# A GELU feed-forward block on one core: the first chunk of x loaded in four quarters over two queues, b1 moved to GpSimd, and every turn of x put ahead of the first pass

## The chip, the cores and the metric

The kernel runs on one core of a Trainium2 chip. The metric is device time in microseconds (us) of one execution; a kernel's time is the median of its runs. The profile is that of one execution.

## What is computed

```python
B, S, D, F = 1, 2048, 448, 1792            # all bfloat16
def reference(x, w1, b1, w2, b2):
    h = jnp.einsum("bsd,df->bsf", x, w1) + b1
    h = gelu(h, approximate=True)
    return jnp.einsum("bsf,fd->bsd", h, w2) + b2
```

2048 tokens, each a row of 448 numbers, go through two matrix products with a GELU between them.

## The kernel before

**Two passes.** The 2048 tokens are cut into 4 chunks of 512, the 1792 hidden units into 14 tiles of 128. The first pass makes, for each of the 56 pairs of chunk and tile, a block of 128 hidden units by 512 tokens in one bank of PSUM, and ScalarE's Gelu (L366) adds b1 and writes it to `g_sb`. The second pass makes 16 output tiles of 128 tokens; VectorE adds b2 (L389), and SyncE stores them (the last part ScalarE). TensorE runs the whole first pass ahead of the second; the order is written out by hand and the five engines run their own lists, tied by semaphores.

**The first pass.** It needs x with its 448 features on the partitions. 448 is three and a half times 128, so x and w1 lie in four row blocks ("slots"), starting at rows 0, 128, 256 and 320. A step is two matmuls (L265) that serve two hidden tiles; in steps of full blocks (128 rows) both use the whole array, in the others each uses a half of it (64 rows). The first 8 hidden tiles have an order of their own, `OPEN`: steps 0 to 3 are slot 0 of tiles 0 to 3, each with one half of the chunk's tokens (256 columns): step 0 tiles 0 and 1, first half; step 1 tiles 2 and 3, first half; steps 2 and 3 the same with the second half. Step 4 is slot 0 of tiles 4 and 5 with all 512 columns, step 5 slot 1 of tiles 0 and 1, step 6 slot 1 of tiles 2 and 3, step 7 slot 0 of tiles 6 and 7. After that come the steps of half the array. What each step waits for is worked out in `opening_waits`: the piece of w1, the parts of x, and the banks of PSUM that parts of x still lie in.

**Turning x.** Chunks 1 to 3 of x are turned by DMA (`load_xT`). Chunk 0 is loaded as it lies, 128 partitions with four tokens each (`xn_sb`, index t = 0 to 3), and TensorE turns it: 16 matmuls of 128x128 against an identity matrix (L248), four for each t, one for each slot. The results lie in PSUM as six parts (`XPARTS`), each with a bank; VectorE or ScalarE casts a part to `xT_sb` once its last turn is done:

- part 0: first half of the tokens (t = 0, 1), slot 0, by VectorE
- part 1: first half, slot 1, by ScalarE
- part 2: first half, slots 2 and 3, by ScalarE
- part 3: second half (t = 2, 3), slot 0, by VectorE
- part 4: second half, slot 1, by VectorE
- part 5: second half, slots 2 and 3, by ScalarE

Turns run part by part: parts 0 to 4 (12 turns) ahead of the pass, part 5 (4 turns) ahead of step 2 (`XLATE`, `EARLY`). Ahead of them stand 12 warm-up matmuls on constants (L238).

**Loads, in the order of their issue on each queue.** SyncE (SP): the two halves of chunk 0 of x (L207, L208); slot 0 of w1 for tiles 4 to 7 (`load_w10(sp, 1)`); slots 1, 2, 3 of w1 for tiles 0 to 7 (L185); slots 0 to 2 (L186) and slot 3 (L189) of the rest of w1; chunks 1 to 3 of x, turned, four transfers each; w2 in two pieces; b2; then the stores. ScalarE: b1, as 14 rows of 128 (L355), then slot 0 of w1 for tiles 0 to 3 (`load_w10(act, 0)`), and behind them its table load (L358). GpSimd: the identity matrix (L224, L226), then 18 rows that fill up b1's block of 32 rows (L231). VectorE turns b1 (four 32x32 transposes, L383, and a cast, L385), behind its three casts of x and ahead of the b2 additions.

Of the kernel before, what the change touches and what calls it, by code (L numbers as in the profile page):

```python
# [11 lines left out]
def bass_standalone__dense_activation_gelu__prompt_kernel(  # L12
# [10 lines left out]
    P = 128  # L23
# [7 lines left out]
    STC = SC // P  # L31
    NFT = F // P

    KROW = [0, 128, 256, 320]
# [24 lines left out]
    W2_PIECES = [(0, 7), (7, 14)]  # L59


    XPARTS = [
        ("d", [(0, 0)]), ("a", [(0, 1)]), ("a", [(0, 2), (0, 3)]),
        ("d", [(1, 0)]), ("d", [(1, 1)]), ("a", [(1, 2), (1, 3)]),
    ]
    XBANK = [0, 2, 4, 5, 6, 7]

    XLATE = 5
    EARLY = 2

    SQ = 32
    NB = 8
# [48 lines left out]
    with ExitStack() as es:  # L121
# [4 lines left out]
        xn_sb = sb("xn_sb", [P, STC, D], BF16)  # L126
        ident = sb("ident", [P, P], BF16)
        act_junk = sb("act_junk", [P, 8], BF16)
        b1n_sb = sb("bin_sb", [SQ, P], BF16)
# [10 lines left out]
        sem_w1r = S_("sem_w1r")  # L140
        sem_w2 = [S_(f"sem_w2_{i}") for i in range(len(W2_PIECES))]
        sem_b2 = S_("sem_b2")
        sem_xn = [S_(f"sem_xn{i}") for i in range(2)]
        sem_b1n = S_("sem_b1n")
        sem_b1x = S_("sem_b1x")
        sem_x = [None] + [S_(f"sem_x{i}") for i in range(1, NSC)]
# [1 line left out]
        sem_xtp = S_("sem_xtp")  # L148
# [22 lines left out]
        def x_part(n, parts):  # L171
# [2 lines left out]
            src = ps[XBANK[n]][:, 0:2 * P * len(parts)]  # L174
            return to, src.rearrange("p (k t) -> p k t", k=len(parts))

        def load_w10(eng, i):
            a, b = W0_PIECES[i]
            with nc.allow_non_contiguous_dma(reason="w1 column pieces"):
                eng.dma_start(w1_sb[:, 0, a * P:b * P], w1[0:P, a * P:b * P]).then_inc(sem_w10[i], 16)  # L180
# [23 lines left out]

        @block.sync
        def _(sp):
            sp.dma_start(xn_sb[:, 0:2, :], x0_view[:, 0:2, :]).then_inc(sem_xn[0], 16)  # L207
            sp.dma_start(xn_sb[:, 2:4, :], x0_view[:, 2:4, :]).then_inc(sem_xn[1], 16)  # L208
            load_w10(sp, 1)
            load_w1(sp)  # L210
            load_xT(sp, 1)
            for c in range(2, NSC):
                load_xT(sp, c)
            for i in range(len(W2_PIECES)):
                load_w2(sp, i)
            sp.dma_start(b2_bc[:, :], b2.partition_broadcast(P)).then_inc(sem_b2, 16)
            for n in range(len(outs) - 1):
                sp.wait_ge(sem_osb, n + 1)
                store(sp, n)
            sp.wait_ge(sem_od, 16 * len(outs))  # L220

        @block.gpsimd
        def _(pool):
            pool.memset(ident[:, :], 0.0).then_inc(sem_id, 1)  # L224
            pool.wait_ge(sem_id, 1)
            pool.affine_select(  # L226
                out=ident[:, :], in_=ident[:, :], compare_op=ALU.not_equal, fill=1.0,
                base=0, pattern=[[-1, P]], channel_multiplier=1,
            ).then_inc(sem_id, 1)

            pool.dma_start(b1n_sb[NFT:SQ, :], w1[0:SQ - NFT, 0:P]).then_inc(sem_b1x, 16)  # L231

        @block.tensor
        def _(pe):
            ones_w = nc.const_aps.tensor(1.0, [P, P], BF16)
            ones_x = nc.const_aps.tensor(1.0, [P, WN], BF16)
            for _i in range(NWARM):
                pe.matmul(ps[0][:, 0:WN], lhsT=ones_w, rhs=ones_x, start=True, stop=True)  # L238
            pe.wait_ge(sem_id, 2)

            def turn_x(n):
                parts = XPARTS[n][1]
                for h, k in parts:
                    if (h, k) in ((0, 0), (1, 0)):
                        pe.wait_ge(sem_xn[h], 16)
                    for t in range(2):
                        col = parts.index((h, k)) * 2 * P + t * P
                        mm = pe.matmul(  # L248
                            ps[XBANK[n]][:, col:col + P],
                            lhsT=xn_sb[:, 2 * h + t, KROW[k]:KROW[k] + P],  # L250
                            rhs=ident[:, :],
                            start=True, stop=True,
                        )
                mm.then_inc(sem_xtp, 1)

            def free(kind, i):
                n = number[kind, i] - NB
                if n >= 0:
                    kind, i = jobs[n]
                    pe.wait_ge(sem_g if kind == "g" else sem_osb, i + 1)  # L260

            def rows(i, k, lo, hi, tokens, start, stop):
                c, ft = order[i]
                t0, t1 = tokens
                return pe.matmul(  # L265
                    bank("g", i)[:, t0:t1],
                    lhsT=w1_sb[lo:hi, k, ft * P:(ft + 1) * P],
                    rhs=xT_sb[lo:hi, k, c * SC + t0:c * SC + t1],
                    start=start, stop=stop,
                )  # L270

            met = set()

            def need(sem, value):
                if (sem.name, value) not in met:
                    pe.wait_ge(sem, value)
                    met.add((sem.name, value))

            def opening_waits(n):

                i, h, m, (t0, t1) = steps[n]
                slots = set(PHASES[h][m])
                for k in sorted(slots):
                    if k > 0:
                        need(sem_w1[k], 16)
                    else:
                        for p, (a, b) in enumerate(W0_PIECES):
                            if a <= i < b:
                                need(sem_w10[p], 16)
                for x, (e, parts) in enumerate(XPARTS):  # L290
                    if XBANK[x] in (i, i + 1) or any(
                        k in slots and t0 <= HALVES[half][0] < t1 for half, k in parts
                    ):
                        need(
                            sem_xTd if e == "d" else sem_xTa, sum(f == e for f, _ in XPARTS[:x + 1])
                        )

            def l1():
                for n, (i, h, m, tokens) in enumerate(steps):
                    if n == EARLY:  # L300
                        for x in range(XLATE, len(XPARTS)):
                            turn_x(x)
                    if n < N_OPEN:
                        opening_waits(n)
                    elif starts[n]:
                        if n == N_OPEN:
                            pe.wait_ge(sem_w1r, 32)
                        for t in (i, i + 1):
                            c, ft = order[t]
                            if c > 0 and ft == 0:  # L310
                                pe.wait_ge(sem_x[c], 16 * NKT)
                            free("g", t)
                    if turn[n] is not None:
                        pe.wait_ge(sem_turn, turned.index(turn[n]) + 1)
                    lower, upper = PHASES[h][m]
                    last = n in ends
                    if h == 2:
                        two = ((0, P, i, lower), (0, P, i + 1, upper))
                    else:
                        two = ((0, HALF, i + 1 - h, lower), (HALF, P, i + h, upper))  # L320
                    for lo, hi, tile, k in sorted(two, key=lambda one: one[2]):
                        mm = rows(tile, k, lo, hi, tokens, starts[n], last)
                        if last:
                            mm.then_inc(sem_l1, 1)
                    if n in turned:
                        mm.then_inc(sem_turn, 1)

            def l2(c):
                pe.wait_ge(sem_g, NFT * (c + 1))
                for n, (j, c0, c1) in enumerate(outs):  # L330
                    if j // STC != c:
                        continue
                    free("o", n)
                    for ft in range(NFT):
                        if j == 0:
                            for i, (a, _) in enumerate(W2_PIECES):
                                if ft == a:
                                    pe.wait_ge(sem_w2[i], 16)
                        mm = pe.matmul(  # L339
                            bank("o", n)[:, 0:c1 - c0],  # L340
                            lhsT=g_sb[:, ft, j * P:(j + 1) * P],
                            rhs=w2_sb[:, ft, c0:c1],
                            start=(ft == 0), stop=(ft == NFT - 1),
                        )
                    mm.then_inc(sem_l2, 1)

            for x in range(XLATE):
                turn_x(x)
            l1()
            for c in range(NSC):  # L350
                l2(c)

        @block.scalar
        def _(act):
            act.dma_start(b1n_sb[0:NFT, :], b1.rearrange("(c p) -> c p", p=P)).then_inc(sem_b1n, 16)  # L355
            load_w10(act, 0)
            zero = nc.const_aps.tensor(0.0, [P, 8], FP32)
            act.activation(act_junk[:, :], zero, ACT.Gelu_apprx_tanh)  # L358
# [62 lines left out]
```

## Time and profile before

| | us |
|---|---|
| runs | 94.48, 94.94, 95.01 (median 94.94) |
| the profiled execution | 93.88 |
| its span, first to last instruction | 92.1 |
| TensorE busy in the span | 89.1 |
| first warm-up starts | 0.79 |
| first turn of x starts | 3.53 |
| step 0 starts | 4.51 |
| last piece of the second pass ends in the chain | 89.88 |

The last four rows are points on the span's own clock, as are all times given as a point below. A matmul's row in the trace starts when the array takes it and ends when its last column has left, so that rows of successive matmuls overlap; the distance from start to start is the pace. A DMA has a row for its issue on the engine that issues it; when its data has landed is told by its semaphore.

Issue and landing of the loads in the opening:

| load | issued by | issue at | landed at |
|---|---|---|---|
| x, t = 0, 1 | SP | 0.75 | 3.39 |
| x, t = 2, 3 | SP | 1.20 | 4.01 |
| b1 | ScalarE | 0.76 | no landing recorded |
| b1's filling rows | GpSimd | 1.67 | 4.93 |
| w1 slot 0, tiles 0 to 3 | ScalarE | 1.43 | 4.36 |
| w1 slot 0, tiles 4 to 7 | SP | 1.66 | 5.19 |
| w1 slot 1, tiles 0 to 7 | SP | 2.13 | 5.96 |
| w1 slot 2, tiles 0 to 7 | SP | 2.60 | 6.60 |
| w1 slot 3, tiles 0 to 7 | SP | 3.08 | 7.63 |
| w1 rest, slots 0 to 2 | SP | 3.55 | 9.96 |
| w1 rest, slot 3 | SP | 4.03 | 10.60 |

### The profile page before, as it was taken

How to read it: one execution, taken by the hardware profiler on the slowest of the kernel's cores; microseconds unless marked ns; L12 is line 12 of the kernel's file. 1: busy time of each engine (PE TensorE's matmuls, PEld its weight loads, DVE VectorE, ACT ScalarE, POOL GpSimd, SP SyncE). 2: the span in 40 equal slices, each digit the busy share in tenths (PEclk: the TensorE clock that was granted, in tenths of full speed). 3: DMA queues.
4: the chain of work that ended last, by engine and by line, in shares of the span. 5: the costliest groups of instructions: out<-in, count | busy, mean ns of one | idle time of the engine just before them, and what ended most of it. 6: DMA issues, size and time to landing. Idle time of an engine off the chain costs nothing.

```text
span 92.1 us, 1498 instructions
## 1 busy us (share of the span) xinstructions
PE 89.1 (97%) x650; PEld 47.2 (51%) x650; DVE 12.2 (13%) x25; ACT 36.6 (40%) x61; POOL 1.4 (1%) x7
## 2 busy tenths in 40 slices
PE   6999999999999999999999999999999999999990
PEld 4664445555555555555545555555555555555570
DVE  0260000000000000000001112222211222222131
ACT  2640999877887779777973000000000000000000
POOL 5000000000000000000000000000000000000000
PEclk9999999999999999999999999999999999999999
DMA  1999988554893000000000111101111110011111
GB/s 24 343 332 333 154 148 73 114 108 74 271 368 104 0 0 4 7 0 0 0 0 0 50 57 50 42 7 50 50 50 50 50 50 29 28 50 50 50 50 50
DMA packets 12562, 7.52 MB, mean 82 GB/s; under 512 B 7171, under 2 KB 12172, under 8 KB 12556
## 3 DMA queue, kind: packets, MB, share of 16 engines
q1 hardware_dynamic: 12208, 7.26, 31.1%
q10 hardware_dynamic: 316, 0.17, 0.6%
q8 instruction: 5, 0.08, 0.3%
q0 software_dynamic: 32, 0.00, 0.1%
q14 instruction: 1, 0.01, 0.0%
HBM read 4.02 MB, written 1.84 MB: 64 GB/s over the span
## 4 chain that ended last, share of the span: by engine, by line
PE 97%; DVE 0%; issue 0%
PE ps L265 46%; PE ps L339 46%; PE ps L238 3%; PE ps L248 1%; DVE out_sb L389 0%
## 5 line engine op out<-in xcount | busy, mean ns | idle before, releaser
L265 PE MATMUL ps<-xT_sb,wi_sb 64*128 64x512 bf16 (+2 forms) x384 | 42.8, 374 | 0.0
L339 PE MATMUL ps<-wo_sb,g_sb 128*128 128x448 bf16 (+2 forms) x238 | 42.6, 341 | 0.0
L366 ACT ACTIVATE g_sb<-ps,bi_f 128x512 bf16<-128x512 f32 x56 | 33.7, 694 | 9.5 <-PE ps L265 9.5
L339 PEld LDWEIGHTS ps<-wo_sb,g_sb 128*128 128x128 bf16 x238 | 22.7, 98 | 20.1 <-issue 0.4
L265 PEld LDWEIGHTS ps<-xT_sb,wi_sb 64*128 64x128 bf16 (+1 forms) x384 | 21.7, 94 | 20.5 <-issue 0.6
L389 DVE TENSOR_TENSOR out_sb<-ps,bo_bc 128x448 bf16<-128x448 f32 (+2 forms) x17 | 10.1, 597 | 73.8 <-PE ps L339 73.8
L238 PE MATMUL ps<-const-bfloat16-1.0 128*128 128x256 bf16 x12 | 2.7, 413 | 0.8 <-PEq L406 0.8
L238 PEld LDWEIGHTS ps<-const-bfloat16-1.0 128*128 128x128 bf16 x12 | 1.6, 140 | 1.4 <-issue 0.8
L358 ACT ACT_TABLE_LOAD x1 | 1.3, 1283 | 1.8 <-issue 1.8
L362 ACT CAST xT_sb<-ps 128x512 bf16<-128x512 f32 (+1 forms) x3 | 1.4, 516 | 1.2 <-PE ps L248 1.2
L378 DVE CAST xT_sb<-ps 128x256 bf16<-128x256 f32 x3 | 1.2, 421 | 4.1 <-PE ps L248 3.9
L248 PEld LDWEIGHTS ps<-ident,xn_sb 128*128 128x128 bf16 x16 | 1.2, 112 | 0.5 <-issue 0.5
L248 PE MATMUL ps<-ident,xn_sb 128*128 128x128 bf16 x16 | 1.4, 244 | 0.0
L383 DVE STREAM_TRANSPOSE bit_sb<-bin_sb 32x32 bf16<-32x32 bf16 x4 | 0.8, 200 | 0.1
L231 POOL DMA_DIRECT2D bin_sb<-in_w_dram x1 | 0.7, 657 | 0.2 <-issue 0.2
L226 POOL TENSOR_SCALAR_AFFINE_SELECT ident<-ident 128x128 bf16<-128x128 bf16 x1 | 0.3, 287 | 0.2 <-POOL ident L224 0.2
L358 ACT ACTIVATE act_junk<-const-float32-0.0 128x8 bf16<-128x8 f32 x1 | 0.2, 209 | 0.0
L224 POOL MEMSET ident<- 128x128 bf16 x1 | 0.2, 204 | 0.3 <-POOLq L406 0.3
L385 DVE CAST bi_f<-bit_sb 128x14 f32<-128x14 bf16 x1 | 0.2, 176 | 0.0
L406 POOL MEMSET const-float32-0.0<- 128x1 f32 x1 | 0.1, 99 | 0.2 <-issue 0.2
L406 POOL MEMSET const-bfloat16-1.0<- 128x1 bf16 x1 | 0.1, 102 | 0.0
L406 POOL MEMSET const-uint8-127<- 128x1 uint8 x1 | 0.1, 102 | 0.0
(1 smaller groups left out, 0.1 us busy)
## 6 DMA issues: line engine op xcount, KB each, us to landing
out_dram<-out_sb SPq DMA_DIRECT2D x15, 112.0 KB, 1.7
wo_sb<-in_w_dram SPq DMA_DIRECT2D x2, 784.0 KB, 6.0
wi_sb<-in_w_dram SPq DMA_DIRECT2D x3, 256.0 KB, 4.0
wi_sb<-in_w_dram SPq DMA_DIRECT2D x1, 576.0 KB, 6.4
xn_sb<-in_x_dram SPq DMA_DIRECT2D x2, 224.0 KB, 2.7
wi_sb<-in_w_dram SPq DMA_DIRECT2D x1, 192.0 KB, 6.6
xT_sb<-in_x_dram SPq DMA_TRANSPOSE x12, 3.6
wi_sb<-in_w_dram ACTq DMA_DIRECT2D x1, 128.0 KB, 2.9
```

What stands on the lines that cost most here:

```text
L231: pool.dma_start(b1n_sb[NFT:SQ, :], w1[0:SQ - NFT, 0:P]).then_inc(sem_b1x, 16)
L238: pe.matmul(ps[0][:, 0:WN], lhsT=ones_w, rhs=ones_x, start=True, stop=True)
L248: mm = pe.matmul(ps[XBANK[n]][:, col:col + P], lhsT=xn_sb[:, 2 * h + t, KROW[k]:KROW[k] + P], rhs=ident[:, :], start=True, stop=True,)
L265: return pe.matmul(bank("g", i)[:, t0:t1], lhsT=w1_sb[lo:hi, k, ft * P:(ft + 1) * P], rhs=xT_sb[lo:hi, k, c * SC + t0:c * SC + t1], start= ...
L339: mm = pe.matmul(bank("o", n)[:, 0:c1 - c0], lhsT=g_sb[:, ft, j * P:(j + 1) * P], rhs=w2_sb[:, ft, c0:c1], start=(ft == 0), stop=(ft == NF ...
L358: act.activation(act_junk[:, :], zero, ACT.Gelu_apprx_tanh)
L362: act.copy(*x_part(n, parts)).then_inc(sem_xTa, 1)
L366: act.activation(g_sb[:, ft, c * SC:(c + 1) * SC], bank("g", i)[:, :], ACT.Gelu_apprx_tanh, bias=b1_f[:, ft:ft + 1], scale=1.0,).then_inc( ...
L378: dve.tensor_copy(*x_part(n, parts)).then_inc(sem_xTd, 1)
L383: dve.transpose(b1t_sb[to, :], b1n_sb[:, to]).then_inc(sem_b1T, 1)
L389: dve.tensor_tensor(out=out_sb[:, j, c0:c1], in0=bank("o", n)[:, 0:c1 - c0], in1=b2_bc[:, c0:c1], op=ALU.add,).then_inc(sem_osb, 1)
L406: nc = _bacc.Bacc("TRN2", target_bir_lowering=False, num_devices=1)
```

## The change

Chunk 0 of x comes as four transfers, one for each t, each with a semaphore: t = 0, 2 and 3 by SP, t = 1 by ScalarE. b1's 14 rows go from ScalarE's queue to GpSimd's, ahead of the filling rows. The turns run tile by tile, the four slots of t = 0, then those of t = 1, 2 and 3, all ahead of the first pass; each t waits for its own quarter. The parts, their banks, their casts and the order of the steps stay. A part is complete with its turn of t = 1 or t = 3.

```diff
-    XLATE = 5
-    EARLY = 2
...
-        sem_xn = [S_(f"sem_xn{i}") for i in range(2)]
+        sem_xn = [S_(f"sem_xn{i}") for i in range(STC)]
...
+        def load_x0(eng, t):
+            eng.dma_start(xn_sb[:, t, :], x0_view[:, t, :]).then_inc(sem_xn[t], 16)
...
         @block.sync
         def _(sp):
-            sp.dma_start(xn_sb[:, 0:2, :], x0_view[:, 0:2, :]).then_inc(sem_xn[0], 16)
-            sp.dma_start(xn_sb[:, 2:4, :], x0_view[:, 2:4, :]).then_inc(sem_xn[1], 16)
+            for t in (0, 2, 3):
+                load_x0(sp, t)
             load_w10(sp, 1)
             load_w1(sp)
...
+            pool.dma_start(b1n_sb[0:NFT, :], b1.rearrange("(c p) -> c p", p=P)).then_inc(sem_b1n, 16)
             pool.dma_start(b1n_sb[NFT:SQ, :], w1[0:SQ - NFT, 0:P]).then_inc(sem_b1x, 16)
...
             pe.wait_ge(sem_id, 2)
-            def turn_x(n):
-                parts = XPARTS[n][1]
-                for h, k in parts:
-                    if (h, k) in ((0, 0), (1, 0)):
-                        pe.wait_ge(sem_xn[h], 16)
-                    for t in range(2):
-                        col = parts.index((h, k)) * 2 * P + t * P
+            for t in range(STC):
+                pe.wait_ge(sem_xn[t], 16)
+                h = t // 2
+                for n, (_, parts) in enumerate(XPARTS):
+                    for b, (_, k) in enumerate(parts):
+                        if parts[b][0] != h:
+                            continue
+                        col = (2 * b + t % 2) * P
                         mm = pe.matmul(
                             ps[XBANK[n]][:, col:col + P],
-                            lhsT=xn_sb[:, 2 * h + t, KROW[k]:KROW[k] + P],
+                            lhsT=xn_sb[:, t, KROW[k]:KROW[k] + P],
                             rhs=ident[:, :],
                             start=True, stop=True,
                         )
-                mm.then_inc(sem_xtp, 1)
+                        if t % 2 == 1 and b == len(parts) - 1:
+                            mm.then_inc(sem_xtp, 1)
...
                 for n, (i, h, m, tokens) in enumerate(steps):
-                    if n == EARLY:
-                        for x in range(XLATE, len(XPARTS)):
-                            turn_x(x)
                     if n < N_OPEN:
...
-            for x in range(XLATE):
-                turn_x(x)
             l1()
...
         @block.scalar
         def _(act):
-            act.dma_start(b1n_sb[0:NFT, :], b1.rearrange("(c p) -> c p", p=P)).then_inc(sem_b1n, 16)
+            load_x0(act, 1)
             load_w10(act, 0)
```

## The prediction

> **What bounds the kernel now.** I read the page's busy shares first, then the chain that ended last in order of time, then the waits of the opening.
>
> ```profile
> span 92.1 us, 1498 instructions
> ...
> PE 89.1 (97%) x650; PEld 47.2 (51%) x650; DVE 12.2 (13%) x25; ACT 36.6 (40%) x61; POOL 1.4 (1%) x7
> ```
>
> TensorE is busy for 97% of the span, so only what moves its first or last work, or opens a hole in it, can move the end.
>
> ```profile
> 0.79 2.72 PE ps L238 x12
> ...
> 3.53 1.05 PE ps L248 x12
> 4.58 0.53 PE ps L265 x4
> 5.11 0.22 PE ps L248 x4
> 5.33 42.02 PE ps L265 x380
> 47.35 42.53 PE ps L339 x238
> ```
>
> Every piece is TensorE's (start, length, line): warm-ups (L238), 12 turns of x (L248), the first four matmuls of the first pass (L265), the last 4 turns, the rest of the first pass, the second pass (L339). From 5.33 to 89.88 there is nothing to win that this change touches. The opening is what it rearranges.
>
> ```profile
> PEld ps L265 <- DMA wi_sb<-in_w_dram: 0.6, 2, 0.3
> PEld ps L248 <- issue: 0.5, 1, 0.5
> ```
>
> These are waits of the weight loads, which run ahead of the matmuls; only part of them is TensorE's loss. I worked that out from matmul starts in the opening's timeline. The warm-ups start 0.213 us apart, the last at 3.09, so its slot ends at 3.30; the first turn starts at 3.53 (the first half of x landed at 3.39): 0.23 lost. The turns start 0.107 apart until 4.01, then 0.056: the array doubles its pace there, while the granted clock reads 1.00 throughout. The twelfth turn's slot ends at 4.42, the first L265 starts at 4.51: 0.09 lost to VectorE's cast. Then starts are on pace, except 0.10 at 7.12, where the matmul shape changes. So 0.23 + 0.09 = **0.32 us** is all that the profiled opening holds for this change, 0.34% of the time.
>
> ```profile
> 6.00 0.13 PEld L265 LDWEIGHTS ps<-xT_sb,wi_sb 128*128 128x128 bf16 x2 [0.30 <-DMA wi_sb<-in_w_dram]
> ...
> 10.64 0.13 PEld L265 LDWEIGHTS ps<-xT_sb,wi_sb 64*128 64x128 bf16 x4 [0.29 <-DMA wi_sb<-in_w_dram]
> ```
>
> These two rows weigh most. w1's second row block was issued at 2.13 and landed at 5.96; its weights load at 6.00 and the matmul runs on pace at 6.04. w1's last columns landed at 10.60, their load is at 10.64, the matmul on pace at 10.68. Both arrive with no slack: what delays them delays TensorE, and if TensorE comes there earlier, it waits.
>
> **The change part by part.** Times are on the profiled execution: 93.88 us, span 92.1 and 1.78 around it. The median of the runs shown is 94.94, 1.06 higher, and the profile doesn't say where that lies; I add the difference worked out here to the median.
>
> *Four quarters.* The same 459 KB move as 512 packets of 896 B in place of 256 of 1,792 B. Among the trace's packets, 1,024 B take 46 ns and 1,792 B take 74; the line through them gives 41 for 896. Per engine that is 32 x 41 - 16 x 74 = 128 ns more. The engines are full from 2.4 us on:
>
> ```profile
> DMA packets 473, 0.58 MB, mean 363 GB/s; under 512 B 67, under 2 KB 473, under 8 KB 473
> ```
>
> (the DMA view of 2.4 to 4.0). So all w1 pieces behind x land **0.13 us** later. By the rows at 6.00 and 10.64, TensorE loses 0.13 at the least if it is on today's schedule. From below: if two queues at 0.75 start the engines sooner, the pieces come earlier by no more than what the slow start (108 GB/s from 1.7 to 2.4) left undone, 0.7 x (1 - 108/363) = 0.49 us.
>
> *SP's third issue.* SP issues three quarters, 0.45 us each (0.75, 1.20, 1.66), in place of two halves, so w10's second piece, w1, the transposes, w2 and b2 are issued 0.45 later. w1's second block would go out at 2.58 and its packets start now at 4.0, 1.9 after issue; the first DMA needed 1.0 from issue to packet. The backlog covers 0.45. The chunk-1 transposes, each 1.2 to 1.9 us of issue, landed by 13.01 and chunk 1 starts at about 14.5: slack 1.5 for 0.45. w2 landed at 28.66 for 47.35. Nothing; without the backlog it would be the 0.45.
>
> *ScalarE issues quarter 1 in place of b1.* b1's issue took 0.64 there, the w1 piece behind it went out at 1.43. A quarter's issue is between 0.36 (that w1 piece) and 0.64, so the piece goes out at 1.15 to 1.43 and landed at 4.36, with L265 first needing it at 4.48. Nothing. The table load behind (1.83 to 3.11) is needed at 9.21; the casts wait for turns. In the Trainium skill, Trainium Kernel Development and Optimization, section Key Constraints, DMAs of the SP, ACT and POOL queues share the same 16 engines, so a second issuer saves issue time only; the 363 GB/s above, over both queues, agrees.
>
> *b1 by GpSimd.* One issue of 0.66 (L231) ahead of the other piece, which then lands at 4.93 + 0.66 = 5.6. VectorE's transposes and cast behind it took 5.17 to 6.28 and come to 5.7 to 6.8. VectorE's three casts stand ahead of that wait in its queue, b2's additions behind it begin near 47. The first Gelu needs b1 at 9.21: 2.4 us of cover. Nothing; only past 2.9 us would it show.
>
> *The order of turns.* Now tile by tile, so part 0's cast waits for the fifth turn, not the second. On today's starts: fifth turn 3.91 to 4.18, cast 4.22 to 4.64, first L265 possible at 4.79 (today's gap from cast end to matmul is 0.15). Sixteen turns without a hole fill TensorE until 4.64. The loss of 0.09 becomes one of up to 0.15; the 4 turns that lay between steps lie ahead. By itself: 6.04 becomes 6.10, +0.06.
>
> *Four waits.* Quarter 0 carries half of the bytes: it lands 8 x (74 - 41) = 0.26 earlier, at 3.13, if quarter 1 doesn't mix in; at 3.45 if their packets alternate. I keep 3.39, since both are issued within 0.01 us. Behind a turn that waits stand all turns and the pass, so the last quarter, landing at **L**, decides. From L a turn starts in 0.14 (3.39 to 3.53), ends 0.22 later, VectorE's cast of part 3 starts 0.04 later and takes 0.42, and 0.15 later the pass's third step runs (its second half of tokens): L + 0.97. Two steps of 0.215 and one of 0.43 follow up to the step that is now at 6.04: L + 1.83. So the delay is **L - 4.21**. Bounds of L: 4.01 (today's second half) + 0.13 = 4.14 from below. If w10's first piece, 131 KB issued at 1.43, goes ahead of the quarter issued at 1.66: 131 KB / 363 GB/s = 0.36 more, 4.50. With its issue's 0.46 not hidden either, 4.97. Today that piece's packets began at 3.31 while x's ended at 3.57, so they overlapped; I take about two thirds of the piece ahead of the quarter, L = 4.40, a delay of **0.19**.
>
> **Sum.** The 0.19 and the 0.13 are not added: a TensorE that is 0.19 late finds w1 there. +0.19: 94.07 on the profiled execution, **95.1** on the median. The tail is untouched.
>
> **The rivals.**
> 1. *The fourth quarter is late.* Mechanism and place as above; it decides over w1's 0.13 from L = 4.34, and passes 0.5% (0.47 us, about what a measurement of this kernel can tell from no change) at L = 4.68. For: it is SP's third issue, behind a foreign piece. Against: the backlog hides issue times elsewhere. With L = 4.8: +0.59, 95.5; at the bound 4.97: +0.76, 95.7.
> 2. *The pace doubles later in the timed runs.* If the array stays at 0.107 per turn through the opening, sixteen turns last 1.71 us and no landing up to 4.6 is waited for; then w1's pieces have slack too, both changes of order cost nothing, and an earlier quarter 0 gives back up to the 0.23: 94.7. For: 1.06 us between profile and median, as much as 2 us more at half pace. Against: not seen here. In the Trainium skill, TensorE: Matmul & The Clock Gate, Part 1, the clock gate's window of some 3.4 us runs freely, and the change of pace shifts by half a microsecond from run to run; the change at 4.01, 3.2 after the first warm-up, agrees.
> 3. *The runs outside the profile wait longer for x.* Some engines' first packets took up to 541 ns, others 74; if the 1.06 us is in part such a wait ahead of the first turn, a quarter that lands first cuts it. With half of 1.06 and the 0.23: 94.2. Against: the other quarters meet the same engines.
> 4. *The quarters land together*, the engines being shared: the change then does not do what it says, and w1's 0.13 alone stays, 95.07. This lies inside the forecast's own band.
>
> **Chances.** Forecast with rival 4: 0.38; rival 1: 0.27; rival 2: 0.22; rival 3: 0.13. Within 0.5% (94.47 to 95.41) fall nearly all of the forecast (0.36) and of rival 2 (0.21), a fifth of rival 1 (0.05) and 0.01 of rival 3: 0.63. Slower: 0.24. Faster: 0.13. The range leaves out about one in ten on each side: down to 94.4, which holds rival 2 and 0.32 below the median and leaves most of rival 3 out; up to 95.6, short of rival 1's bound.
>
> **What would show it.** L248's 16 turns in one piece, with TensorE's first L265 at 4.8 to 5.0; the xn landings at 3.4, 3.4, about 4.0 and 4.4; a 0.2 us hole ahead of the third step; the wi_sb waits at 6.0 and 10.6 gone if TensorE is later, or longer by 0.13 if not; b1's cast near 6.8. If the first turn is well ahead of 3.53 and w1's last columns land ahead of 10.5, my floor is wrong; if L passes 4.7, rival 1.

## The result, and the profile after

The changed kernel takes 95.32 us (median of 23 runs) against 94.93 for the kernel before (23 runs); the ratio is **1.0054**, 95% interval 1.003 to 1.0077. Seven of the changed kernel's 23 executions, and none of the 23 of the kernel before, lie near 97 us; the ratios here and below leave such executions out, and the profile of the changed kernel is of one of them (97.68), so its lines show the mechanism at its largest. How much the change costs depends on how it is taken: the ratio makes it 0.51 us (of 94.93), the two medians differ by 0.39, and the changed kernel's other 16 executions average 95.14 against 94.82 for all 23 of the kernel before, 0.32 more. The forecast was 95.1, a difference of 0.19.

The page's lines of the changed kernel:

```profile
span 95.9 us, 1500 instructions
...
PE 91.0 (95%) x650; PEld 47.9 (50%) x650; DVE 12.2 (13%) x25; ACT 36.6 (38%) x61; POOL 1.9 (2%) x8
...
PEclk9996699999999999999999999999999999999999
```

TensorE is still busy for most of the span, but the last line, the granted clock in 40 slices, holds two slices at 6 near 7 to 12 us, which the kernel before doesn't have. The chain in order of time (start, length, what):

```profile
1.66 4.75 DMA xn_sb<-in_x_dram
6.41 0.05 issue
6.46 0.40 PE ps L250 x4
6.85 44.23 PE ps L268 x384
51.08 42.53 PE ps L339 x238
```

The chain no longer starts with the warm-ups. It starts with the fourth quarter of x, issued as SP's third transfer at 1.66 and landed at **6.41**; behind it hang the last four turns and the whole first pass. The second pass (L339) takes 42.53, to the last digit what it took before. TensorE's rows in the opening's timeline (start, length, engine, line, with the idle time ahead):

```profile
3.29 1.30 PE L250 MATMUL ps<-ident,xn_sb 128*128 128x128 bf16 x12
6.46 0.40 PE L250 MATMUL ps<-ident,xn_sb 128*128 128x128 bf16 x4 [1.86 <-DMA xn_sb<-in_x_dram]
```

The first turn does start earlier, at 3.29 in place of 3.53: quarter 0 landed at 3.15, quarters 1 and 2 at 3.32 and 3.76, and twelve turns run without a hole. Then TensorE waits. By stretches (borders, length, busy time and count of each engine, granted clock, DMA share, GB/s):

```profile
3.40:4.20 0.80, 0.80 (x10) 0.80 (x9) 0.13 (x1) 0.03 (x1) 0.00 (x0) 1.00 0.81 203
4.20:5.00 0.80, 0.39 (x6) 0.22 (x3) 0.29 (x1) 0.80 (x2) 0.00 (x0) 1.00 0.91 203
```

and a later stretch of the same kernel:

```profile
7.65:11.20 3.55, 3.55 (x12) 1.04 (x11) 0.75 (x4) 0.00 (x0) 0.00 (x0) 0.52 1.26 252
```

The first two stretches in the kernel before:

```profile
3.40:4.20 0.80, 0.77 (x10) 0.70 (x10) 0.26 (x1) 0.05 (x1) 0.00 (x0) 1.00 1.06 328
4.20:5.00 0.80, 0.80 (x12) 0.67 (x10) 0.66 (x3) 0.80 (x2) 0.00 (x0) 1.00 0.97 329
```

Two things are to be seen. From 3.4 us on, for some 1.6 us, the loads move 203 GB/s where they moved 328; 345 were moved just ahead of that. All but five of the fourth quarter's 128 packets had started by 4.33; the last four started at 5.86 to 5.98, and one packet of the quarter that began at 4.20 took 1.65 us, to 5.85. And from 7.65 to 11.2 the granted clock is 0.52: twelve matmuls run in 3.55 us, and those of 512 columns start 0.427 apart where full pace is 0.216.

### The profile page after: what moved, and what is told of

Same layout as the page of the kernel before. It is cut to its first block, busy times and chain, and to the rows that moved or that the text cites. A ratio compares the mean times of both kernels' runs of the same rounds, so it can differ in the third digit from the quotient of the medians.

```text
span 95.9 us, 1500 instructions
## 1 busy us (share of the span) xinstructions
PE 91.0 (95%) x650; PEld 47.9 (50%) x650; DVE 12.2 (13%) x25; ACT 36.6 (38%) x61; POOL 1.9 (2%) x8
## 2 busy tenths in 40 slices
DMA packets 12854, 7.52 MB, mean 78 GB/s; under 512 B 7207, under 2 KB 12464, under 8 KB 12848
## 3 DMA queue, kind: packets, MB, share of 16 engines
HBM read 4.02 MB, written 1.84 MB: 61 GB/s over the span
## 4 chain that ended last, share of the span: by engine, by line
PE 91%; DMA 5%; SPq 1%; DVE 0%; issue 0%
PE ps L268 46%; PE ps L339 44%; DMA xn_sb<-in_x_dram 5%; SPq L176 1%; PE ps L250 0%; DVE out_sb L387 0%
## 5 line engine op out<-in xcount | busy, mean ns | idle before, releaser
L268 PE MATMUL ps<-xT_sb,wi_sb 64*128 64x512 bf16 (+2 forms) x384 | 44.4, 379 | 0.0
L339 PE MATMUL ps<-wo_sb,g_sb 128*128 128x448 bf16 (+2 forms) x238 | 42.6, 342 | 0.0
L268 PEld LDWEIGHTS ps<-xT_sb,wi_sb 64*128 64x128 bf16 (+1 forms) x384 | 22.2, 95 | 21.7 <-issue 2.8
L339 PEld LDWEIGHTS ps<-wo_sb,g_sb 128*128 128x128 bf16 x238 | 22.7, 98 | 20.1 <-issue 0.4
L231 POOL DMA_DIRECT2D bin_sb<-in_b_dram x1 | 0.6, 640 | 0.2 <-issue 0.2
```

Source lines behind the costliest of these rows:

```text
L231: pool.dma_start(b1n_sb[0:NFT, :], b1.rearrange("(c p) -> c p", p=P)).then_inc(sem_b1n, 16)
L268: return pe.matmul(bank("g", i)[:, t0:t1], lhsT=w1_sb[lo:hi, k, ft * P:(ft + 1) * P], rhs=xT_sb[lo:hi, k, c * SC + t0:c * SC + t1], start= ...
L339: mm = pe.matmul(bank("o", n)[:, 0:c1 - c0], lhsT=g_sb[:, ft, j * P:(j + 1) * P], rhs=w2_sb[:, ft, c0:c1], start=(ft == 0), stop=(ft == NF ...
```

## The experiments

Three theories were set against each other at first: **L** (the fourth quarter lands late because of its place in the queue), **O** (the new order of turns costs), **G** (b1 on GpSimd disturbs the loads), and later **S** (any GpSimd transfer does), **P** (whoever stands third on SP's queue lands late), **N**, **T** and **B** (what sets off the fall in the loads' rate: packets, time or bytes), **Q** (what is queued behind the quarter holds it up) and **C** (the clock).

### The order of turns alone

Made from the kernel after, with the loads of before (`load_x0` moves a half here, and the turns wait for a half):

```diff
-            for t in (0, 2, 3):
-                load_x0(sp, t)
+            for h in range(2):
+                load_x0(sp, h)
...
-            pool.dma_start(b1n_sb[0:NFT, :], b1.rearrange("(c p) -> c p", p=P)).then_inc(sem_b1n, 16)
...
-            load_x0(act, 1)
+            act.dma_start(b1n_sb[0:NFT, :], b1.rearrange("(c p) -> c p", p=P)).then_inc(sem_b1n, 16)
```

> The kernel before with the new order of turns alone; x in two halves and b1 on ScalarE as before. Theory L (the fourth quarter lands late and TensorE waits for it): no quarter, the second half lands near 4.0, so 94.9 to 95.0, ratio within 0.999 to 1.002. Theory O (the order of turns itself costs, by casts that start later): the whole loss, ratio 1.004 or more, step 0 at 4.8 or later. Theory G (GpSimd's second transfer disturbs the loads): ratio 1.000.

Measured: 1.0002 (0.9967 to 1.0037). The second half landed at 3.99, step 0 started at 4.94 in place of 4.51, and the time did not grow by it. Theory O falls. What the profiled execution (94.75) waited for is w1's slot 1, SP's fourth transfer here as before:

```profile
2.14 4.66 DMA wi_sb<-in_w_dram
6.80 0.05 issue
6.85 41.32 PE ps L270 x374
```

### The new loads alone

Made from the kernel before, with the loads of after and the turns in the old order:

```diff
                 for h, k in parts:
-                    if (h, k) in ((0, 0), (1, 0)):
-                        pe.wait_ge(sem_xn[h], 16)
                     for t in range(2):
+                        if k == 0:
+                            pe.wait_ge(sem_xn[2 * h + t], 16)
```

> The kernel before with the new loads alone (four quarters, the second by ScalarE, b1 by GpSimd) and the old order of turns. Theory L: the last quarter lands as late as in the changed kernel, ratio 1.004 to 1.008, and single executions 2 us longer as in it. Theory O: ratio 1.000. Theory G: as theory L, since b1 is on GpSimd here.

Measured: **1.0109** (1.0061 to 1.0156), the fourth quarter landed at 5.91. The loads carry the loss.

### b1 on GpSimd alone

```diff
+            pool.dma_start(b1n_sb[0:NFT, :], b1.rearrange("(c p) -> c p", p=P)).then_inc(sem_b1n, 16)
             pool.dma_start(b1n_sb[NFT:SQ, :], w1[0:SQ - NFT, 0:P]).then_inc(sem_b1x, 16)
...
-            act.dma_start(b1n_sb[0:NFT, :], b1.rearrange("(c p) -> c p", p=P)).then_inc(sem_b1n, 16)
             load_w10(act, 0)
```

> The kernel before with one thing changed: b1 is issued by GpSimd ahead of the filling rows. Theory G: ratio 1.004 or more, packets of the x and w1 loads that take over 0.3 us from 3.2 us on, some executions 2 us longer. Theories L and O: ratio 0.999 to 1.001, no execution 2 us longer.

Measured: 1.0024 (0.999 to 1.0058): not told apart from nothing. The x halves landed at 3.69 and 4.39, where they landed at 3.39 and 4.01 before; w1's first piece now went out at 0.75, beside the first of them. It did show packets above 0.3 us, as theory G said, but so does the next run, without b1 on GpSimd.

### The change without b1 on GpSimd

```diff
-            pool.dma_start(b1n_sb[0:NFT, :], b1.rearrange("(c p) -> c p", p=P)).then_inc(sem_b1n, 16)
...
             load_x0(act, 1)
             load_w10(act, 0)
+            act.dma_start(b1n_sb[0:NFT, :], b1.rearrange("(c p) -> c p", p=P)).then_inc(sem_b1n, 16)
```

> The changed kernel with b1 taken from GpSimd and issued by ScalarE behind w1's first piece. Theory G: the loss is gone, ratio 0.998 to 1.001, fourth quarter landed by 4.2. Theory L (place in the queue): ratio 1.004 to 1.008 as in the changed kernel, fourth quarter landed at 4.4 or later. Theory O: as theory L in time, but with the fourth quarter by 4.2 and step 0 at 4.8 or later.

Measured: **1.0119** (1.0076 to 1.0162); the fourth quarter landed at 5.85. Its chain:

```profile
1.66 4.19 DMA xn_sb<-in_x_dram
5.85 0.05 issue
5.89 0.40 PE ps L249 x4
6.29 3.01 PE ps L267 x17
```

The same picture as in the changed kernel. Theory G falls.

### No transfer on GpSimd's queue at all

```diff
+            pool.memset(b1n_sb[:, :], 0.0).then_inc(sem_b1x, 1)
...
-            pool.dma_start(b1n_sb[NFT:SQ, :], w1[0:SQ - NFT, 0:P]).then_inc(sem_b1x, 16)
...
             load_w10(act, 0)
+            act.wait_ge(sem_b1x, 1)
+            act.dma_start(b1n_sb[0:NFT, :], b1.rearrange("(c p) -> c p", p=P)).then_inc(sem_b1n, 16)
```

once on the changed kernel, once on the kernel before; b1's own transfer leaves its old place in both.

> The changed kernel without any transfer on GpSimd's queue: the filling rows are a memset, b1 is issued by ScalarE behind w1's first piece. Theory S (GpSimd's transfer slows single engines from 3.2 us on, and the fourth quarter waits for the slowest engine): no packets over 0.3 us between 3.0 and 5.0, the fourth quarter (issued at 1.66) lands by 4.6, ratio 0.997 to 1.002. Theory P (it is the third place on SP's queue, whoever stands there, since that transfer lands at 5.2 to 6.4 in all six traces so far): lands at 5.2 or later, ratio 1.004 to 1.012.

> The kernel before without any transfer on GpSimd's queue, b1 by ScalarE behind w1's first piece. Theory S: w1's second piece of slot 0 (issued at 1.66, landed at 5.19 before) lands by 4.7, w1's slot 1 by 5.6, ratio 0.994 to 1.000. Theory P: it lands at 5.2 or later, ratio 0.998 to 1.002.

Measured: 1.0078 (1.0036 to 1.0119) with the quarter landed at 5.23, and 1.0011 (0.9976 to 1.0047). Stretches of the second, the kernel before without GpSimd's transfer:

```profile
3.40:4.20 0.80, 0.47 (x5) 0.41 (x5) 0.00 (x0) 0.00 (x0) 0.00 (x0) 1.00 1.13 375
4.20:5.00 0.80, 0.80 (x10) 0.80 (x9) 0.42 (x1) 0.50 (x2) 0.00 (x0) 1.00 0.75 149
```

The fall is there too, to 149 GB/s, with single packets of up to 1.1 us, and no GpSimd transfer. Theory S falls. But here it comes about when x has landed (3.69 and 4.39), and what lands late is w1's slot 1 (6.84), SP's fourth transfer, which the kernel's median doesn't show. The third landed at 4.71, so theory P's 5.2 was missed here; the time, which P put at no change, was not.

### The fourth quarter by ScalarE

```diff
-            for t in (0, 2, 3):
+            for t in (0, 2):
...
             load_x0(act, 1)
+            load_x0(act, 3)
             load_w10(act, 0)
```

alone, and with no transfer on GpSimd's queue.

> The changed kernel with the fourth quarter issued by ScalarE ahead of w1's first piece, no longer third on SP's queue. Theory P: it lands by 4.3, w1's piece that is now third on SP's queue lands at 5.2 or later, ratio 0.997 to 1.002. Theory S: the fourth quarter, issued 0.5 us sooner, ends ahead of most of the slow packets and lands at 3.9 to 4.5, the ratio 0.998 to 1.004; the slow packets are still there.

> Both: fourth quarter by ScalarE ahead of w1's first piece, and no transfer on GpSimd's queue (b1 by ScalarE third). Theory S: all loads on time, the first turn near 3.3, 0.2 us less than before: ratio 0.995 to 0.999. Theory P: as the run with the fourth quarter on ScalarE alone, within 0.002 of it.

All of x landed by 4.10 and 3.94, as both theories said, but neither got the time: 1.0097 (1.0054 to 1.0139) for the second; for the first there is no interval, its six executions took 95.7 (two) and 97.2 to 97.7 (four). Now w1's two pieces of slot 0 stand third, one on each queue, and land at 6.19 and 6.38 (6.33 and 6.49 in the second). The chain of the first:

```profile
1.67 4.71 DMA wi_sb<-in_w_dram
6.38 0.05 issue
6.42 2.77 PE ps L268 x16
```

The wait has only moved from x to w1: sixteen turns are done, and step 0 waits for its weights.

### Third place without any quarter

```diff
             sp.dma_start(xn_sb[:, 0:2, :], x0_view[:, 0:2, :]).then_inc(sem_xn[0], 16)
-            sp.dma_start(xn_sb[:, 2:4, :], x0_view[:, 2:4, :]).then_inc(sem_xn[1], 16)
             load_w10(sp, 1)
+            sp.dma_start(xn_sb[:, 2:4, :], x0_view[:, 2:4, :]).then_inc(sem_xn[1], 16)
```

on the kernel before; 128 rows of 1,792 B as before.

> The kernel before with SP's second and third transfer exchanged: the second half of x goes third, issued at 1.66, nothing else changed. Theory P (third place on SP's queue): it lands at 5.2 or later, ratio 1.004 to 1.012, with no quarter and no move of b1. Theory N: it is packets 384 to 512, ahead of the fall, so it lands at 4.4 to 4.8; ratio 1.000 to 1.004, and w1's slot 1 lands at 6 or later.

Measured: **1.018** (1.0124 to 1.0236), more than the whole change, though its six executions are spread from 96.0 to 98.7.

```profile
1.66 4.90 DMA xn_sb<-in_x_dram
6.56 0.04 issue
6.60 0.40 PE ps L248 x4
```

The half lands at 6.56. Theory P's landing holds and N falls: the fall came after 370 data packets, where the others had 457 to 574. Neither the size of the quarters nor b1 is needed for the loss: to go third on SP's queue, issued at 1.66 in place of 1.20, is enough.

### x in one piece

```diff
-            sp.dma_start(xn_sb[:, 0:2, :], x0_view[:, 0:2, :]).then_inc(sem_xn[0], 16)
-            sp.dma_start(xn_sb[:, 2:4, :], x0_view[:, 2:4, :]).then_inc(sem_xn[1], 16)
+            sp.dma_start(xn_sb[:, :, :], x0_view[:, :, :]).then_inc(sem_xn[0], 16)
...
-                    if (h, k) in ((0, 0), (1, 0)):
-                        pe.wait_ge(sem_xn[h], 16)
+                    if (h, k) == (0, 0):
+                        pe.wait_ge(sem_xn[0], 16)
```

> The kernel before with chunk 0 of x as one transfer of 128 rows of 3,584 B in place of two. So far the loads fall from about 350 to under 260 GB/s for about a microsecond once 457 to 574 data packets have started, at 3.2 to 4.3 us, with 410 to 742 KB. Theory N (the number of packets decides): 128 packets fewer in front, so the fall comes at 4.7 to 5.2 us with near 980 KB. Theory T (it is a time after the start): at 3.2 to 4.3 us. Theory B (bytes): at 410 to 742 KB. Time: x lands near 4.0 in one piece, so ratio 1.000 to 1.004 by each.

Measured: 0.9986 (0.9953 to 1.0019), from five executions; the other seven of the twelve took 95.9 to 97.0, so this is no better version. x landed at 4.10. There was no clear fall at all up to 5.8 us:

```profile
3.40:4.20 0.80, 0.10 (x1) 0.00 (x0) 0.00 (x0) 0.00 (x0) 0.00 (x0) 1.00 1.09 365
4.20:5.00 0.80, 0.76 (x8) 0.79 (x9) 0.35 (x1) 0.14 (x1) 0.00 (x0) 1.00 0.92 309
```

So T and B fall with it, and N's fall at 4.7 to 5.2 is missing too: neither a time nor a number of bytes or of packets alone sets it off. What stands third on SP, w1's slot 1 here, still landed only at 6.12.

### w1 held back

```diff
             for t in (0, 2, 3):
                 load_x0(sp, t)
+            sp.wait_ge(sem_xn[3], 16)
```

> The changed kernel with SP waiting for the fourth quarter ahead of w1's other pieces. Theory Q (w1's packets behind it hold the fourth quarter up): it lands at 4.0 to 4.4. Theory N: it is packets 512 to 640 and lands at 5.0 or later although nothing is queued behind it. Time by both: w1's slot 1 lands 2.5 to 4 us after the wait, so slower, ratio 1.01 to 1.03.

Measured: 1.0267 (1.0215 to 1.0318), slower, as foreseen. The fourth quarter landed at 5.04 with nothing behind it on SP's queue; 179 GB/s were moved from 3.4 to 4.2 and 12 after that. Theory Q explains at most the rest, 5.04 against 5.23 to 6.41. N's 5.0 or later was met here, though N had its number of packets wrong in the two runs above.

### Work in the hole

```diff
             for t in range(STC):
+                if t == 3:
+                    for _i in range(5):
+                        pe.matmul(ps[1][:, 0:WN], lhsT=ones_w, rhs=ones_x, start=True, stop=True)
                 pe.wait_ge(sem_xn[t], 16)
```

> The changed kernel with five more warm-up matmuls on constants between the turns of the third and the fourth quarter, 0.5 to 1.1 us of TensorE work in the hole. Theory C (executions of about 97 us are those in which the hole makes the granted clock fall to half for 3.4 us, costing 1.7): no execution at 97 among all, the others as the changed kernel or up to 0.5 us longer, ratio 1.004 to 1.010. If the executions at 97 come from something else, they stay at about a third.

Measured: 1.008 (1.0053 to 1.0106), six executions of 95.31 to 95.71, none near 97.

```profile
4.24 0.72 PE L245 MATMUL ps<-const-bfloat16-1.0 128*128 128x256 bf16 x5
6.19 0.40 PE L253 MATMUL ps<-ident,xn_sb 128*128 128x128 bf16 x4 [1.24 <-DMA xn_sb<-in_x_dram]
```

The quarter landed at 6.15, nearly as late as in the changed kernel's profile, and the granted clock did not fall. That agrees with theory C, and so do the clock rows of the two traces. But with seven of 23 as the rate, six of six without a long execution would come about in one case of nine by chance, so the count doesn't prove it. And a fall of the clock is not the whole account. Two other long executions were profiled, of the new loads alone (97.21) and of x in one piece (96.67), and they show another thing: TensorE is at half pace from its first matmul on, with matmuls of 512 columns still 0.427 apart, until about 9.4 and 9.2 (the page of neither has a clock row). Nor does every hole bring the clock down. In the run with the second half of x in third place (96.22) TensorE waits a little longer than in the changed kernel (2.05 us against 1.86), and everything behind the wait is at full pace:

```profile
6.60 0.40 PE L248 MATMUL ps<-ident,xn_sb 128*128 128x128 bf16 x4 [2.05 <-DMA xn_sb<-in_x_dram]
```

Of the changed kernel's seven long executions only one was profiled, so which of the two the other six had is not known. Executions of 96.7 us or more came in most versions with a wait in the opening (five of twelve without GpSimd's transfers, two of six with the new loads alone), and once in 69 further executions of the kernel before (96.73).

## Why the prediction was right, and where it wasn't

**The bound was right.** Everything is settled in the opening, and one point of it carries the time: the start of step 5, the one the prediction put at "6.04" and at "L + 1.83". Over the profiled executions of ten of the fourteen kernels, time less that start is a constant, 87.84 to 87.93:

| kernel | fourth quarter (second half) landed | step 5 starts | time | difference |
|---|---|---|---|---|
| before | 4.01 | 6.04 | 93.88 | 87.84 |
| order of turns alone | 3.99 | 6.85 | 94.75 | 87.90 |
| before, no GpSimd transfer | 4.39 | 7.23 | 95.10 | 87.87 |
| b1 on GpSimd alone | 4.39 | 7.30 | 95.19 | 87.89 |
| after, no GpSimd transfer | 5.23 | 7.29 | 95.21 | 87.92 |
| after, b1 on ScalarE | 5.85 | 7.52 | 95.45 | 87.93 |
| after, hole filled | 6.15 | 7.82 | 95.71 | 87.89 |
| fourth quarter by ScalarE | 4.10 | 7.74 | 95.66 | 87.92 |
| the same, no GpSimd transfer | 3.94 | 7.86 | 95.79 | 87.93 |
| third place, no quarter | 6.56 | 8.37 | 96.22 | 87.85 |
| new loads alone | 5.91 | 9.23 | 97.21 | 87.98 |
| x in one piece | 4.10 | 8.46 | 96.67 | 88.21 |
| after | 6.41 | 8.47 | 97.68 | 89.21 |
| after, w1 held back | 5.04 | 8.28 | 98.04 | 89.76 |

The last four rows leave the line, each by what still goes wrong behind that start: half pace up to 9.4 and 9.2, the stretch at half clock, a wait for w1. The stretch at half clock, 3.41 us long, costs half of that, 1.7 us; 0.4 of it lies ahead of step 5 and 1.3 behind.

**The step that failed is L.** I put the fourth quarter's landing at 4.40, with 4.97 as the upper bound; in the five traces with the quarter in that place and w1 behind it, it landed at 5.23 to 6.41. The bound was made of bytes over a rate of 363 GB/s and of an issue time. The row that would have told it was on the table: SP's third transfer of the kernel before, issued at the same 1.66, landed at 5.19. The runs show what that row meant: in 13 of 14 traces SP's third transfer, whatever it carried, landed 3.4 to 4.9 us after its issue, where the first and second landed 2.4 to 3.4 after theirs:

| third on SP | kernel | landed |
|---|---|---|
| w1 slot 0, second piece | before; order of turns; b1 on GpSimd | 5.19; 5.40; 5.46 |
| the same | before, no GpSimd transfer | 4.71 (the fourth, 6.84) |
| the same | fourth quarter by ScalarE; without GpSimd transfer | 6.19; 6.33 |
| w1 slot 1 | x in one piece | 6.12 |
| second half of x | third place, no quarter | 6.56 |
| fourth quarter | after; new loads; b1 on ScalarE | 6.41; 5.91; 5.85 |
| the same | no GpSimd transfer; filled; w1 held back | 5.23; 6.15; 5.04 |

In the kernel before a load with cover stands there (needed at 5.60, landed at 5.19). The change puts one there that has none.

**The formula held, its price didn't.** "L + 1.83" gives 7.68 for L = 5.85 and 7.52 was measured, 7.98 for 6.15 and 7.82 was measured: a turn starts 0.05 after the landing, not 0.14, and the steps up to step 5 take 0.07 less. It holds for an array at full pace behind the landing; for L = 5.23, where the pace doubles only at 6.30, step 5 came at 7.29, not 7.06. By the forecast's own sum these landings would have been a loss of 1.0 us or more. It was 0.3 to 0.5, and the traces speak for rival 2 as the reason, in both kernels: the array doubles its pace at 4.02 in the profile that I worked from, but at 4.80, 6.38 and 6.52 in the traces of the order of turns alone and of the two kernels with the old loads and GpSimd's part changed. In the last two, TensorE reaches step 5 at 7.23 and 7.30 although x landed by 4.39; in the first it is at 6.85, held by w1's slot 1, which landed at 6.80. Twelve turns that took 1.05 in the profile of the kernel before take 1.44 in that of b1 on GpSimd alone:

```profile
3.82 1.44 PE ps L249 x12
5.26 0.85 PE ps L266 x4
6.11 0.43 PE ps L249 x4
```

There it is 3.48 us from the first turn to step 5. With that stretch behind a first turn at 3.53, the kernel before would reach step 5 at 7.01 and take 94.9, which is its median; this is an estimate, since of the kernel before only the execution of 93.88 was profiled. The forecast added a delay counted from that short execution to the median. In a typical one the wait for the fourth quarter lies mostly where work at half pace, or a wait for w1, lay before. So two terms were off, in opposite directions: the landing by 0.8 to 2.0 us, and the slack of a typical execution by about 1 (step 5 at 7.01 in place of 6.04). That 0.19 came out near 0.3 to 0.5 is luck. By the sign that the prediction set itself, L past 4.7, it was rival 1 that happened: it named the mechanism and its place, and its 95.5 is nearer than the forecast's 95.1 to what the ratio gives (1.0054 x 94.93 = 95.44); the median of 95.32 lies about midway.

On the clock, the prediction cited the Trainium skill, TensorE: Matmul & The Clock Gate, Part 1, for a change of pace that moves by half a microsecond. The traces here show more: in the seven in which matmul starts show the moment in the opening it lies between 3.50 and 6.52, and in two long executions it lies at about 9.2 and 9.4, after starts of the warm-ups that agree within 0.02. The same page, Why this matters for your kernels, asks for no idle gaps above about 3 us; here a hole of 2 us (4.4 to 6.46) stood ahead of a stretch of 3.41 us at half clock (7.68 to 11.09). The measurement decides: less than the page's gap was enough, though not always, since no stretch at half clock followed the 2.05 us of the run with the half in third place.

**Point by point.** The first turn: I kept 3.53, it came at 3.29, close to the lower bound that I gave for quarter 0 (3.13; it landed at 3.15). That gain of 0.24 is then waited away. *Four quarters* at 0.13 for more packets: w1's last columns landed at 11.13 against 10.60, 0.5 later, but nobody waited for them. *SP's third issue*: I wrote that the backlog hides the 0.45 and looked only at what comes behind the quarters, not at the quarter's own place. *b1 by GpSimd* at nothing: right, 1.0024 with an interval that holds 1; b1's cast came at 8.32, ahead of the first Gelu. *The order of turns* at 0.06 by itself: right in the time, 1.0002. *ScalarE's queue* at nothing: right for w1's first piece (3.96). Rivals 3 and 4 didn't come about: the time rose, and the quarters landed one after another.

**What stays open** is why that transfer is late. In eleven of the fourteen traces the rate falls from about 350 to 150 to 200 GB/s for about a microsecond, in the other three the transfer was late without such a fall, and single packets take up to 1.9 us in place of 0.04 to 0.08. Not GpSimd's transfers, not a fixed time, and not a fixed number of bytes or packets set it off. Transfers third on ScalarE's queue were late as well (6.38, 6.49). But place and moment of issue are not told apart: every third transfer here was issued at 1.65 to 1.67. GpSimd's first, issued at 1.66 to 1.69 with 3.5 or 4.5 KB, landed only at 4.69 to 6.12 in the eleven traces that have one, which speaks for the moment as much as for the place. No run issued a third transfer earlier or later, and that it is a limit on what a queue holds ready was not tried.

## What to carry to other kernels

Price a moved transfer by the landing of whatever stood in the same place of the same queue, not by bytes over the rate: the trace of the kernel before had it. Before splitting a load to get its head sooner, count what then stands third in the queue (here, what is issued at about 1.66), and give that place to something with a microsecond or two of cover. And where a profile is one execution, look at what in it varies from run to run (here the moment at which the array doubles its pace) before taking its slack as the slack of all.

## What the runs showed that I had not expected

- The time of an execution is the start of one step plus 87.9 us, over ten kernels within 0.09 us.
- A hole of about 2 us on TensorE was followed by 3.41 us at half the granted clock in the changed kernel's profile, 1.7 us in all; one of the same length in another run was not.
- The pace of the array doubled at 3.50 to 6.52 us in executions whose first matmul started at the same time, and at about 9.2 and 9.4 in two long ones. With the old loads, 4.02 goes with 93.88 us and 6.38 and 6.52 with 95.10 and 95.19.
- A load that lands 0.8 to 2.0 us later than my 4.40 cost 0.3 to 0.5 us here. That TensorE is at half pace in the same stretch in many executions explains it; it is argued from the traces of other versions, not shown on this kernel's own typical execution.
